# Reordering steps in a linear-attention and MLP block: tail scalings, low parts, hidden chunks and one `up` are issued at other places

## The chip, the cores and the metric

The kernel runs on one core of one Trainium2 chip, as a single program. The metric is the device time of one execution in microseconds (us); lower is better. The times of the kernel before are three executions, 745.16, 745.22 and 745.53 us, with a median of 745.22 us. One more execution was profiled.

## What is computed

One transformer block on 2048 tokens of width 640 (32 heads of 20), in float32:

```python
sa, ca, ga, sb, cb, gb = six rows of silu(c) @ w_mod
h = layernorm(x) * (1 + ca) + sa
x = x + ga * attention(h)          # below
h = layernorm(x) * (1 + cb) + sb
x = x + gb * (relu(h @ w1 + b1) ** 2 @ w2 + b2)     # w1: 640 x 1728

# attention: q, k, v = h @ wqkv, for each head
phi(t) = [softmax(t @ w_phi), softmax(-t @ w_phi)]
o = phi(q) (phi(k)^T v) / (phi(q) sum(phi(k)) + 1e-6),  then o @ wo
```

## The kernel before, in words

**Number format.** Each float32 operand of a large product is held as two parts in the matmul format: a high part (`hi`, an ACT copy that rounds) and a low part (`lo`, line 94: a DVE subtraction, original minus high part). A product is then three matmuls, high by high, high by low and low by high (`three`, line 91). So nearly every matmul operand is made by one ACT step and one DVE step after it, and PE waits for both.

**Stages.** (1) Up to about 248 us: weights are folded, layer norm, k, q and v are projected token tile by token tile, and `phi(k)^T v` is summed. (2) From there to 374 us: the query side, called the attention loop here, `for j in range(NB)` (line 1254), eight turns of 256 tokens each, that is two tiles of 128 tokens. (3) From 374 us to the end: the MLP, again eight turns `j` of 256 tokens (line 1666), each with seven inner turns `n` over pairs of 128-wide chunks of the hidden width 1728.

**The attention loop.** For each tile t of 128 tokens:

- `load_e` (line 899) reads the stored exponentials of the tile from DRAM, 640 KB, issued on SP's queue, into a buffer that an earlier tile must have left.
- `e_prod` (915): on DVE a product with the sums of phi(k) (line 919) and a reduction (921), then four small steps on POOL (924 to 928).
- `e_recip` (930): on DVE the reciprocal (933), which waits for the last POOL step, and one product (934).
- `e_scale` (961) is `e_tail` and then `e_main`. `e_tail` (938) scales the last two heads (line 944; on DVE for tiles 0 to 5, on POOL from tile 6 on). `e_main` (950) scales the other thirty heads on DVE (line 955).
- PE then does `tail_turn` (967: transposes of the tails into the single PSUM bank tagged `tp`), `tail_num` (974), `tr_e` (982: transposes of the main part) and `num` (992: products with the masked `phi(k)^T v`, in two banks and the `tp` bank), ACT takes the high parts (`num_hi`, 1010), and `num_lo` (1014) takes the low parts, from turn 2 on by DVE straight from PSUM (line 95 in the trace). The bank `tp` is free for the next `tail_turn` only after the last of those. `do_wo` (1027) is the output product, four pieces a turn (`i` the tile, `h` the half), of 15 matmuls each.

`todo_` and `turns` (1257 to 1262) say after how many matmuls of which piece of `do_wo` the steps of the next turn come in. PE, DVE, ACT and POOL run in the written order here; SP's order is left to the scheduler of the framework. Ahead of the loop lines 1224 to 1251 do the same for tiles 0 to 4 by hand; `kv_mask5` and `kv_masks` (889, 892) are DVE products that make the masked `phi(k)^T v`.

**Into the MLP.** `t2(0, d)` (1137) makes chunk d of the five chunks of `h` for the first 256 tokens: two ACT steps (lines 404 and 405) and one DVE subtraction (95). `prep` is one hidden weight: `p_hi`, an ACT copy (1083); `p_lo`, a DVE subtraction; `p_load`, the load of a later weight on SP. In the last turns of the attention loop they are issued in groups.

**The MLP.** `up(j, f)` (1362) is 15 matmuls into one of two banks, a relu on ACT (1380) and a square on DVE (1381). `split_a(j, n)` (1397) splits the squares of a pair into high (ACT, 1404 and 1410) and low parts (DVE); `down(0)` and `down(1)` multiply the pair before by w2 into the banks `acc` and `acc3x`. In a turn (j, n) the order on PE is `up(2n)`, `down(0)`, `up(2n+1)`, `down(1)`, where the downs are those of turn n-1. Between them stand calls of `prep` and `layer` (1643), which does the layer norm of the next 256 tokens in pieces; one of the pieces is `turn` (1172), a DVE transpose, after which `t2` of the next tokens can run. All engines are in the written order, SP too for j = 0.

Of the kernel before, what the change touches and what calls it, by code (L numbers as in the profile page):

```python
# [56 lines left out]
def kernel(  # L57
# [436 lines left out]
    def do_q(t, *between):  # L494
        q_out(t, proj("q", t, *between))
# [465 lines left out]
    def e_scale(t):  # L961
        e_tail(t)
        e_main(t)
# [151 lines left out]
    def p_lo(n=1):  # L1115
        for _ in range(n):
            if todo["lo"]:
                prep_lo(*todo["lo"].pop(0))

    def new(tag):  # L1120
        return lambda nm: wslot(nm, tag)

# [103 lines left out]
    e_prod(0)  # L1226
    e_prod(1)
    e_recip(0)
    e_scale(0)
    e_recip(1)  # L1230
    load_e(3)
    do_q(q0 + 2, (1, 0, kv_diags))
    e_tail(1)
    kv_mask5()
    e_main(1)
    kv_masks()
    e_prod(2)
# [6 lines left out]
    e_prod(3)  # L1244
    e_recip(2)
    e_recip(3)
    e_scale(2)
    load_e(5)
    e_scale(3)
    load_e(6)  # L1250
    e_prod(4)
    SPREAD, SUMS = {1: 1, 3: 2}, {3: 1, 4: 2}
# [1 line left out]
    for j in range(NB):  # L1254
        nxt = j + 1 < NB
        b, c = 2 * j + 5, 2 * j + 6
        turns = {1: ((0, 0, 11), (0, 0, 15), (0, 1, 4), (0, 1, 15)), 6: ((0, 1, 2), (0, 1, 8), (0, 1, 15), (1, 0, 15)),
                 0: ((0, 1, 4), (0, 1, 10), (1, 0, 3), (1, 0, 15))}.get(j, ((0, 0, 6), (0, 0, 11), (0, 0, 15), (0, 1, 15)))
        todo_ = (lambda: tail_turn(j + 1), lambda: tail_num(j + 1), lambda: tr_e(j + 1, range(3)), lambda: tr_e(j + 1, (3, 4)))

        def hooks(i, h):
            return [(at, f) for (i_, h_, at), f in zip(turns, todo_) if nxt and (i, h) == (i_, h_)]
        if j == 4:
            load_x1(0)
            load_dealt(0)
        if j < 5:
            p_load()
        if j == 5:
            q_chain(KEPT + 3, False)
        else:  # L1270
            e_prod(b)
        e_recip(b - 1)
        e_scale(b - 1)
        if j == 6:
            mod_sum(5, gate_b)
            spread_row(1, gb_b)
        load_e(b + 2)
        do_wo(j, 0, 0, *hooks(0, 0))
        if j - 1 in SPREAD:
            exps(EQ[KEPT + SPREAD[j - 1]])  # L1280
        if j == 5:
            exps(EQ[KEPT + 3])
            q_sums(KEPT + 3)
            e_prod(b)
        do_wo(j, 0, 1, *hooks(0, 1))
        if j == 7:
            t2(0, 0)
            t2(0, 1)
        if j == 4:
            ln0 = ln_dealt(0)  # L1290
            next(ln0)
            next(ln0)
        if j == 6:
            next(ln0)
            turn(0, 0)
            turn(0, 1)
        if 1 <= j < 6 and j != 4:
            p_hi()
        if j == 5:
            next(ln0)  # L1300
        if j in SUMS:
            q_sums(KEPT + SUMS[j])
        e_prod(c)
        if j != 5:
            e_recip(b)
            e_scale(b)
        do_wo(j, 1, 0, *hooks(1, 0))
        if j == 7:
            t2(0, 2)
            t2(0, 3)  # L1310
        if nxt:
            num(j + 1)
            num_hi(j + 1)
        if j == 4:
            next(ln0)
            next(ln0)
            next(ln0)
        if j == 5:
            p_hi()
        do_wo(j, 1, 1, b=8)  # L1320
        if j == 7:
            t2(0, 4)
        if not nxt:
            do_wo(j, 1, 1, a=8)
        if nxt:
            do_wo(j, 1, 1, a=8, b=11)
            num_lo(j + 1)
            do_wo(j, 1, 1, a=11)
        if j == 5:
            e_recip(b)  # L1330
            e_scale(b)
        if j in SPREAD:
            q_chain(KEPT + SPREAD[j], False)
        load_e(c + 2)
        if j:
            plus_x(j - 1)
        if j == 5:
            p_lo(4)
            p_load(4)
        if j == 6:  # L1340
            p_hi(4)
            p_lo(5)
            p_load(3)
        if j == 7:
            p_load(2)
    order.__exit__(None, None, None)


# [257 lines left out]
            out_(*r, u[:, at : at + m])  # L1606
            at += m

    def prep(n):
        p_hi(n)  # L1610
        p_lo(n)
        p_load(n)

    prev = None
    LN2 = {}

# [49 lines left out]
    for j in range(NB):  # L1666
        if j <= PLAIN:
            if j:
                by_hand.__exit__(None, None, None)
            by_hand = tc.manual_schedule(engines={ET_.PE, ET_.DVE, ET_.Activation, ET_.Pool} | ({ET_.SP} if j != 1 else set()))  # L1670
            by_hand.__enter__()
        for n in range(NP):
            down = lambda k: prev and (down_plain if plain(*prev) else down_pair)(*prev, k)
            twice = not plain(j, n)
            m = NP * j + n - NP - 1
            if (j, n) == (NB - 1, NP - 1):
                for k in range(2):
                    up(j, 2 * n + k)
                    split_a(j, n, (k,))
                break  # L1680
            done = j - 1 if j and prev else None
            up(j, 2 * n)
            if prev and not plain(*prev):
                split_s(*prev)
            down(0)
            if j < PLAIN:
                layer(j + 1, 2 * n, None if j else 0)
            if 0 < m < NP - 2:
                t_split(m - 1)
            if m == -1:  # L1690
                t_load(0)
            if (j, n) == (PLAIN, 0):
                t_fetch(4)
            if j >= PLAIN:
                if n == 5 + (j == PLAIN) - (j == NB - 1):
                    for i in range(2):
                        add_bias(j, i)
                layer(j + 1, 2 * n)
            prep(next(PREPS, 0))
            if j == 0:  # L1700
                layer(j + 1, 2 * n, 1)
# [24 lines left out]
            if j == NB - 1 and n == 1:  # L1726
                for k in range(NP - LAST, NP - 1):
                    plain_load(k)
            if j == NB - 1 and n == 3:
                for k in range(NP - LAST, NP - 1):  # L1730
                    plain_split(k)
            if j == NB - 1 and n == NP - 2:
                for i in range(2):
                    by_gate(Y[j][i], Y[j][i], slice(0, D))
                    add(Y[j][i], Y[j][i], XR[j, i])
            up(j, 2 * n + 1)
            if j >= PLAIN and n == 0:
                down(1)
            split_a(j, n)
            if twice:  # L1740
                sums(j, n)
            if j < PLAIN or n:
                down(1)
            if m == NP + 1:
                t_split(NP - 2)
            ahead = (j, n) == (0, 3)
            if ahead:
                layer(j + 1, 2 * n + 1)
            prep(next(PREPS, 0))
            if n == 0 and j:  # L1750
                end(j - 1, "4", 1, L)
                end(j - 1, "x", 1, R)
            if n == (2 if j > PLAIN else 1 if j == PLAIN else 0) and j:
                finish(j - 1, j >= PLAIN)
            if not ahead:
                layer(j + 1, 2 * n + 1)
            if (j, n) == (0, 4):
                nc.vector.tensor_tensor(bb, bb, gb_b, op=ALU.mult)
            if 0 <= m < NP - 2:
                t_sums(m)  # L1760
            if m == NP - 2:
                t_split(m - 1)
            if 0 < m + 1 < NP - 1:
                t_load(m + 1)
            if m == NP - 1:
                for i in range(2):
                    add_bias(j - 1, i)
            if j == NB - 1 and n == NP - LAST:
                first_combos(j)
            prev = j, n  # L1770
# [78 lines left out]
```

## Time and profile before

| | us |
|---|---|
| median of the timed executions | 745.22 |
| the profiled execution, its own time | 746.29 |
| its span, first to last instruction | 744.6 |
| PE busy | 735.9 |
| DVE busy | 600.1 |
| ACT busy | 453.6 |
| POOL busy | 168.3 |

The span is 1.7 us shorter than the profiled execution's own time, which in turn is 1.1 us above the median. PE, the engine of the matmuls, is busy for 99% of the span, and it is idle for the rest. In the rows of the profile, PE is the matmul, PEld its weight load, and a row of the timeline gives the start, the duration of a group of like instructions, the engine, the line of the kernel, what is written and read, and the count; brackets give the idle time of the engine before it and who ended it. Matmuls overlap, and their ends are modelled, so the distance from one start to the next is the surer figure.

### The profile page before, as it was taken

Reading aid. Unit: us, or ns where it says so; the run is one execution under the profiler, and the core shown is the slowest. Engines: PE = TensorE matmul, PEld = TensorE weight load, DVE = VectorE, ACT = ScalarE, POOL = GpSimd, SP = SyncE. Lnnn points to the kernel's source line nnn. Section 1 sums busy time; section 2 is a strip of 40 time slices with the busy share of each in tenths; the row PEclk is TensorE's granted clock in tenths of the full one; section 3 lists DMA queues with packets and bytes.
Section 4 is the critical chain, followed back from the end, with each engine's and each line's share of the span. In section 5 each row is a group of like instructions: output and inputs, shape, how many; then the busy total and the mean of one; then the engine's idle time right before and its main releaser. Section 6 shows DMA issues by size and latency. Waiting matters only on the chain.

```text
span 744.6 us, 16806 instructions
## 1 busy us (share of the span) xinstructions
PE 735.9 (99%) x6594; PEld 717.8 (96%) x6594; DVE 600.1 (81%) x1092; ACT 453.6 (61%) x1059; POOL 168.3 (23%) x357
## 2 busy tenths in 40 slices
PE   9999999999999999999999999999999999999997
PEld 8999999999999989988999999999999999999997
DVE  6598988988999999999666778877776776777765
ACT  5767666677853365666686567565664747557331
POOL 3000101001000357647203040231321313222110
PEclk9999999999999999999999999999999999999999
DMA  8912341333431345644984477997766777767451
GB/s 312 361 40 96 124 133 57 123 127 108 142 108 72 116 155 182 154 122 122 219 254 151 143 224 250 293 299 186 214 183 183 221 184 226 206 176 206 136 156 36
DMA packets 58421, 126.55 MB, mean 170 GB/s; under 512 B 7022, under 2 KB 16062, under 8 KB 58342
## 3 DMA queue, kind: packets, MB, share of 16 engines
q1 hardware_dynamic: 38110, 79.21, 32.5%
q0 software_dynamic: 17504, 40.90, 21.8%
q10 hardware_dynamic: 2727, 5.37, 1.9%
q8 instruction: 52, 0.85, 0.5%
q14 instruction: 28, 0.22, 0.1%
HBM read 100.80 MB, written 29.89 MB: 176 GB/s over the span
## 4 chain that ended last, share of the span: by engine, by line
PE 81%; DVE 10%; DMA 3%; POOL 2%; ACT 2%; issue 1%; SPq 0%; ACTq 0%; DVEq 0%; POOLq 0%
PE up L85 24%; PE acc L85 17%; PE pk L85 9%; PE pv L85 9%; PE pq L85 8%; PE acc3x L85 5%; PE pwo L85 3%; DVE dn L921 3%; DVE scr L919 2%; DVE ezb L955 2%; PE kvp L488 1%; DMA raw_q<-in_wq 1%; DMA xx<-a 1%; DMA ring_b<-td_b 1%; PE ta L393 1%
## 5 line engine op out<-in xcount | busy, mean ns | idle before, releaser
L85 PE MATMUL up<-h,w 128*128 128x256 f32 x1640 | 204.9, 277 | 0.1
L85 PEld LDWEIGHTS up<-h,w 128*128 128x128 f32 x1640 | 196.7, 188 | 0.7 <-DVE h L95 0.5
L1380 ACT ACTIVATE ft<-up,b_t 128x256 f32<-128x256 f32 x104 | 49.0, 471 | 96.9 <-PE up L85 96.6
L85 PE MATMUL acc<-w,ra 128*128 128x384 f32 x452 | 97.5, 335 | 0.0
L1381 DVE TENSOR_TENSOR ft<-ft 128x256 f32<-128x256 f32 x104 | 43.9, 422 | 42.9 <-ACT ft L1380 41.5
L85 PE MATMUL pwo<-wo,ot 128*128 128x384 f32 (+1 forms) x480 | 78.0, 313 | 0.0
L85 PE MATMUL pq<-wq,hT 128*128 128x384 f32 (+1 forms) x480 | 76.0, 313 | 0.0
L85 PE MATMUL pk<-wk,hT 128*128 128x384 f32 (+1 forms) x480 | 73.8, 310 | 0.0
L85 PEld LDWEIGHTS acc<-w,ra 128*128 128x128 f32 x452 | 72.7, 188 | 0.8 <-DVE ra L95 0.6
L85 PEld LDWEIGHTS pq<-wq,hT 128*128 128x128 f32 x480 | 71.5, 188 | 0.7 <-issue 0.5
L85 PEld LDWEIGHTS pwo<-wo,ot 128*128 128x128 f32 x480 | 69.5, 188 | 2.7 <-issue 2.7
L85 PE MATMUL pv<-wv,hT 128*128 128x384 f32 (+1 forms) x480 | 72.0, 307 | 0.0
L85 PEld LDWEIGHTS pk<-wk,hT 128*128 128x128 f32 x480 | 70.7, 188 | 1.2 <-DVE hT L95 0.7
L85 PEld LDWEIGHTS pv<-wv,hT 128*128 128x128 f32 x480 | 70.4, 188 | 0.0
L95 DVE TENSOR_TENSOR ra<-ft,ra 128x384 fp32r<-128x384 f32 (+2 forms) x86 | 36.9, 449 | 32.6 <-ACT ra L1404 19.4
L1490 POOL DMA_DIRECT2D ring_a<-td_a x34 | 18.5, 543 | 116.5 <-PE acc L85 106.3
L1404 ACT ACTIVATE ra<-ft 128x384 fp32r<-128x384 f32 x48 | 25.2, 526 | 28.4 <-DVE ft L1381 22.4
L85 PE MATMUL acc3x<-w,ra 128*128 128x256 f32 x231 | 39.5, 278 | 0.0
L85 PEld LDWEIGHTS acc3x<-w,ra 128*128 128x128 f32 x231 | 37.2, 188 | 0.0
L479 DVE TENSOR_REDUCE sk<-ek 128x64 f32<-128x1280 f32 x16 | 23.7, 1484 | 13.4 <-ACT ek L474 9.1
L1395 DVE TENSOR_TENSOR ft<-ft 128x128 f32<-128x128 f32 x136 | 33.3, 287 | 1.2
L370 POOL TENSOR_SCALAR sma<-sma 128x2 f32<-128x2 f32 x6 | 2.3, 376 | 132.8 <-ACT xb L369 132.8
(264 smaller groups left out, 1443.9 us busy)
## 6 DMA issues: line engine op xcount, KB each, us to landing
ring_c<-td_c POOLq DMA_DIRECT2D x34, 384.0 KB, 3.9
ring_a<-td_a POOLq DMA_DIRECT2D x34, 384.0 KB, 3.4
ring_b<-td_b POOLq DMA_DIRECT2D x34, 256.0 KB, 3.4
esp<-eq SPq DMA_DIRECT2D x12, 640.0 KB
el<-esp SPq DMA_DIRECT2D x12, 640.0 KB
rw<-in_w SPq DMA_DIRECT2D x23, 320.0 KB
wm<-in_w_mod SPq DMA_DIRECT2D x20, 320.0 KB
xb<-in_x SPq DMA_DIRECT2D x8, 640.0 KB
```

The source lines that it names most:

```text
L85: nc.tensor.matmul(o, a, b, start=first and i == 0, stop=last and i == len(terms) - 1, skip_group_check=skip,)
L95: (eng or nc.vector).tensor_tensor(out_lo, full, hi.bitcast(F32), op=ALU.subtract)
L393: nc.tensor.transpose(p[:, i * P : (i + 1) * P], src, ident)
L479: nc.vector.tensor_reduce(s, heads(flat(e)), axis=AX.X, op=ALU.add)
L919: nc.vector.tensor_tensor(z, flat(ET[t]), flat(zb), op=ALU.mult)
L921: nc.vector.tensor_reduce(dn.rearrange("p s h -> p (s h)"), heads(z), axis=AX.X, op=ALU.add)
L955: nc.vector.tensor_tensor(EU[t][:, :, :120].rearrange("p u (s h d) -> p s u h d", s=2, d=DH), ET[t][:, :, :600].rearrange("p s (u h d) -> ...
L1380: nc.scalar.activation(r, p, AF.Relu, bias=b1_t[:, f : f + 1])
L1381: nc.vector.tensor_tensor(r, r, r, op=ALU.mult)
L1395: nc.vector.tensor_tensor(t[:, o], t[:, a], t[:, b], op=op)
L1404: nc.scalar.activation(a[:, 0, :3], t[:, :3], AF.Copy)
L1490: nc.gpsimd.dma_start(RING[j, n, r], TD[n][r].bitcast(F32R))
```

## The change

Six groups of edits, all of them of order; no instruction is added or taken away.

1. Tiles 0 and 1: `e_tail(0)`, `kv_mask5` and `e_tail(1)` come ahead of `e_main(0)`; `load_e(3)`, which takes the buffer that `e_main(0)` reads, comes after it.
2. Tiles 2 and 3: both tails come ahead of both mains.
3. Turn j = 4 of the attention loop: `e_main(13)` comes after `num_lo(5)` and not ahead of it. In the other turns the lines are written anew with the same order.
4. `t2(0, 0)` comes at the end of turn 6, each of the other chunks one piece of `do_wo` sooner in turn 7, the last one ahead of the last piece. One of the weights (high part, low part) and one load go from the end of turn 6 to the end of turn 7.
5. MLP, turn (0, 1): `up(0, 3)` comes ahead of `down(0)`.
6. MLP, turn (0, 5): one `prep` comes after the relu of `up(0, 11)`; turn (0, 4): the piece of `layer` (a `turn`) comes ahead of a `prep`.

```diff
@@ tiles 0 to 3 @@
     e_recip(0)
-    e_scale(0)
+    e_tail(0)
+    do_q(q0 + 2, (1, 0, kv_diags))
+    kv_mask5()
     e_recip(1)
+    e_tail(1)
+    e_main(0)
     load_e(3)
-    do_q(q0 + 2, (1, 0, kv_diags))
-    e_tail(1)
-    kv_mask5()
     e_main(1)
...
     e_recip(3)
-    e_scale(2)
+    e_tail(2)
+    e_tail(3)
+    e_main(2)
     load_e(5)
-    e_scale(3)
+    e_main(3)
@@ attention loop @@
         do_wo(j, 0, 0, *hooks(0, 0))
+        if j == 7:
+            t2(0, 1)
...
         if j == 7:
-            t2(0, 0)
-            t2(0, 1)
+            t2(0, 2)
+            t2(0, 3)
...
             e_recip(b)
-            e_scale(b)
+            e_tail(b)
+            if j != 4:
+                e_main(b)
         do_wo(j, 1, 0, *hooks(1, 0))
         if j == 7:
-            t2(0, 2)
-            t2(0, 3)
+            t2(0, 4)
...
-        do_wo(j, 1, 1, b=8)
-        if j == 7:
-            t2(0, 4)
...
+        do_wo(j, 1, 1, b=11)
         if nxt:
-            do_wo(j, 1, 1, a=8, b=11)
             num_lo(j + 1)
-            do_wo(j, 1, 1, a=11)
+        if j == 4:
+            e_main(b)
+        do_wo(j, 1, 1, a=11)
...
         if j == 6:
-            p_hi(4)
-            p_lo(5)
-            p_load(3)
+            p_lo()
+            t2(0, 0)
+            p_hi(3)
+            p_lo(3)
+            p_load(2)
         if j == 7:
-            p_load(2)
+            prep(1, 3)
@@ MLP @@
             up(j, 2 * n)
+            ahead = (j, n) == (0, 1)
+            if ahead:
+                up(j, 2 * n + 1)
...
-            prep(next(PREPS, 0))
+            parts = next(PREPS, 0)
+            late_ = (j, n) == (0, 5)
+            if not late_:
+                prep(parts)
...
-            up(j, 2 * n + 1)
+            if not ahead:
+                up(j, 2 * n + 1)
...
+            if late_:
+                prep(parts)
             split_a(j, n)
...
-            ahead = (j, n) == (0, 3)
-            if ahead:
+            sooner = (j, n) in ((0, 3), (0, 4))
+            if sooner:
                 layer(j + 1, 2 * n + 1)
```

More of the change, by code (lines that the diff above doesn't have):

```diff
@@ L1118, in p_lo, with prep @@
                 prep_lo(*todo["lo"].pop(0))
+    def prep(n, m=None):
+        p_hi(n)
+        p_lo(n)
+        p_load(n if m is None else m)
     def new(tag):
@@ L1319 @@
             p_hi()
-        do_wo(j, 1, 1, b=8)
-        if j == 7:
-            t2(0, 4)
-        if not nxt:
-            do_wo(j, 1, 1, a=8)
+        do_wo(j, 1, 1, b=11)
         if nxt:
-            do_wo(j, 1, 1, a=8, b=11)
             num_lo(j + 1)
-            do_wo(j, 1, 1, a=11)
+        if j == 4:
+            e_main(b)
+        do_wo(j, 1, 1, a=11)
         if j == 5:
@@ L1607, in last_downs @@
             at += m
[L1609 to L1612, printed above, removed]
     prev = None
@@ L1754 @@
                 finish(j - 1, j >= PLAIN)
-            if not ahead:
+            if not sooner:
                 layer(j + 1, 2 * n + 1)
```

## The prediction, made before the changed kernel was run

> **What bounds the kernel now.** I read the page first, then who PE's weight loads waited for between 236 and 420 us (the stretch that the change touches), then busy times by window, then the timeline engine by engine around each of PE's waits.
>
> ```profile
> span 744.6 us, 16806 instructions
> PE 735.9 (99%) x6594; PEld 717.8 (96%) x6594; DVE 600.1 (81%) x1092; ACT 453.6 (61%) x1059; POOL 168.3 (23%) x357
> PE 81%; DVE 10%; DMA 3%; POOL 2%; ACT 2%; issue 1%; SPq 0%; ACTq 0%; DVEq 0%; POOLq 0%
> ```
>
> PE is busy for 99% of the span, and yet a tenth of the chain that ended last runs over DVE. Both are true: there is a stretch where DVE has no pause either and PE is only just not held up. The second view says what ended the pauses of the weight loads, the third where DVE is full.
>
> ```profile
> PEld tail L971 <- DVE ut L944: 1.1, 2, 0.8
> PEld tail L971 <- POOL rn L1195: 0.9, 1, 0.9
> ...
> 248.27:309.44 61.17, 60.62 (x451) 54.66 (x450) 59.09 (x71) 31.78 (x73) 34.73 (x62) 1.00 0.51 158
> 309.44:338.42 28.98, 28.53 (x214) 25.55 (x212) 28.22 (x33) 17.88 (x41) 15.14 (x30) 1.00 0.58 138
> ```
>
> In the window rows the fifth number is DVE's busy time: 59.1 of 61.2 us, then 28.2 of 29.0. So from 248 to 338 us the query side runs at DVE's pace, and a wait of PE taken away there comes back at the next place where PE needs DVE, unless DVE itself gets that result ready sooner. That is the question for edits 1 to 3. After 374 us PE sets the pace, and there a wait taken away stays away.
>
> **Edits 1 and 2, tails of tiles 0 to 3 ahead of the mains.** PE's rows around the four tail transposes:
>
> ```profile
> 256.74 0.27 PE L971 MATMUL tail<-ident,ut 128*80 128x128 f32 x1
> 257.45 0.31 PE L971 MATMUL tail<-ident,ut 128*80 128x128 f32 x1 [0.44 <-DVE ut L944]
> 268.36 0.69 PE L971 MATMUL tail<-ident,ut 128*80 128x128 f32 x2
> ...
> 309.60 0.38 PE L971 MATMUL tail<-ident,ut 128*80 128x128 f32 x2
> ```
>
> An undisturbed pair takes 0.38 us, its second start 0.38 - 0.27 = 0.11 after the first. At 257 us the second came 0.71 after the first: 0.60 lost. At 268 us the pair took 0.69: 0.31 lost. With both tails in front of the mains (1.40 us each, below) both are ready in time, and PE gains 0.9 us here.
>
> Does it keep them? The next tails in front of which PE has little room come with turn 2, where the transposes need the bank `tp`, which DVE's third low part frees:
>
> ```profile
> 309.03 0.41 DVE L95 TENSOR_TENSOR ot<-numc,ot 128x256 fp32r<-128x256 f32 x1
> ...
> 306.67 3.10 PE L85 MATMUL pwo<-wo,ot 128*128 128x256 f32 x21
> ...
> 334.88 3.09 PE L85 MATMUL pwo<-wo,ot 128*128 128x256 f32 x21
> 338.57 0.39 PE L971 MATMUL tail<-ident,ut 128*80 128x128 f32 x2 [0.60 <-DVE ot L95]
> ...
> 335.44 1.45 DVE L955 TENSOR_TENSOR ezb<-eq,dn 128x1200 f32<-128x1200 f32 x1
> 338.01 0.41 DVE L95 TENSOR_TENSOR ot<-numc,ot 128x256 fp32r<-128x256 f32 x1
> ```
>
> At 338 us, where PE surely waited, it started 338.57 - 338.42 = 0.15 after the low part's end. At 309 us the low part ended at 309.44, so PE could start at 309.59, and it did at 309.60. PE waited there for nothing, but with a room of 0.01 us. A PE that comes 0.9 us earlier waits 0.9 there. DVE is not sooner, since the edits leave it the same work and it goes from one step to the next without a pause. So I cost edits 1 and 2 at no gain, and ask how much later they make DVE:
>
> ```profile
> 252.94 0.59 POOL L928 TENSOR_TENSOR dd<-dd,dn 128x32 f32<-128x32 f32 x2
> 254.69 1.78 POOL L928 TENSOR_TENSOR dd<-dd,dn 128x32 f32<-128x32 f32 x2
> ...
> 254.96 1.40 DVE L955 TENSOR_TENSOR ezb<-el,dn 128x1200 f32<-128x1200 f32 x1
> 256.50 0.35 DVE L933 RECIPROCAL dd<-dd 128x32 f32<-128x32 f32 x1
> ```
>
> The reciprocal of tile 1 waits for POOL's pair of additions. The pair took 0.59 us for tile 0, with DVE in a reduction, and 1.78 for tile 1, from 254.69 to 256.47, when `e_main(0)` ran beside it from 254.96 to 256.36. With `e_main(0)` moved behind the reciprocal, the pair should take 0.59 and end at 255.28, so the reciprocal starts about 1.2 us sooner and `e_main(0)` 1.2 later. DVE, free of the first tail at 254.96, then waits until 255.28, 0.32 us less the small mask product that now lies in between, where it waited 0.14 before (256.36 to 256.50). So it comes between nothing and 0.2 later; I take 0.1. The Trainium skill (SBUF — State Buffer, "Who interferes with whom") says that a VectorE instruction with two SBUF inputs and a GpSimd one that reads SBUF lock each other out, whichever starts first holding the port to its end; by that rule the second addition is held by `e_main(0)`, as the row has it, and comes free by the edit. If the slow pair had another cause, DVE would stand 1.2 us more, which is a rival below.
>
> SP: `load_e(3)` now waits for `e_main(0)` in its later place.
>
> ```profile
> 256.39 2.78 SPq L905 DMA_DIRECT2D el<-esp  x2
> 256.40:260.40 4.00, 3.56 (x30) 3.24 (x30) 3.83 (x7) 0.96 (x4) 0.58 (x3) 1.00 0.63 192
> ...
> 262.34 1.48 DVE L919 TENSOR_TENSOR scr<-el,zb 128x1280 f32<-128x1280 f32 x1
> ```
>
> It was issued at 256.39, when `e_main(0)` ended, and will be at about 257.6. In the 4.00 us behind the issue 192 GB/s x 4.00 = 768 KB moved, more than its 655 KB (128 x 1280 x 4 bytes), so I let it take 4 us: there at 261.6, and needed at 262.34. The cover is 0.7 us. If it is gone, every us counts on DVE's chain. The other loads are issued well ahead of use.
>
> **Edit 3, low part ahead of the scaling in turn 4.** From the product group `pwo` to the tails is 309.60 - 306.67 = 2.93 us undisturbed and 338.57 - 334.88 = 3.69 at 338 us: 0.76 lost, because `e_main(13)` stood in front of the low parts. With it behind, they end about 1.4 us sooner, at 337.0; PE could start at 337.2 and comes at 338.57 - 0.76 = 337.81. The whole 0.76 goes, with 0.6 us to spare. Next in line is `e_main(13)`: it ends where the low parts ended, and PE needs it only behind the tail steps that follow 338.57. Edits 1 to 3 together: 0.76 - 0.10 = **0.65 us**.
>
> **Edit 4, the chunks of `h`.** Rows of PE, then of ACT and DVE:
>
> ```profile
> 374.19 6.44 PE L85 MATMUL up<-h,w 128*128 128x256 f32 x45
> 380.47 1.01 PE L85 MATMUL acc<-w,ra 128*128 128x384 f32 x3
> ...
> 382.54 1.86 PE L85 MATMUL up<-h,w 128*128 128x256 f32 x15
> 384.24 0.68 PE L85 MATMUL acc<-w,ra 128*128 128x384 f32 x3
> ...
> 366.58 1.37 ACT L1083 ACTIVATE w<-rawt 128x640 fp32r<-128x640 f32 x2 [0.40 <-ACT at L1051]
> 370.09 0.39 ACT L1051 ACTIVATE at<-pwo 128x256 f32<-128x256 f32 x1 [0.52 <-PE pwo L85]
> ...
> 376.12 0.43 DVE L95 TENSOR_TENSOR h<-xm,h 128x256 fp32r<-128x256 f32 x1 [0.52 <-ACT h L405]
> ```
>
> One `up` takes 384.24 - 382.54 = 1.70 us, three 5.10; the first three took 380.47 - 374.19 = 6.28. Of the 1.18 us more I count **1.0** as waits for chunks 3 and 4 and the rest as a slightly slower pace of 45 matmuls. The fifth chunk's low part was ready at 376.55; PE needs it 13 matmuls after its start, at 374.19 + 13 x 1.70 / 15 = 375.66. ACT gets one weight copy less ahead of it (0.65 us, from 1.37 for two) and fills the 0.52 us in which it waited for PE with a chunk: 1.15 sooner, 375.4. That is 0.25 us in front of the need. Bounds: 0.7 if the chunk still comes 0.3 late, 1.18 if the pace goes too. The moved copy stands in front of the first relu; the moved load of an MLP weight is issued some us later, with two loads of the next tokens behind it on SP, all used some us after that.
>
> **Edit 5, `up(0, 3)` ahead of the first downs.** The first product group took 1.01 us instead of 0.68: **0.33** lost on the split of the first pair. It now comes a whole `up`, 1.70 us, later.
>
> ```profile
> 378.91 0.47 ACT L1380 ACTIVATE ft<-up,b_t 128x256 f32<-128x256 f32 x1 [0.60 <-PE up L85]
> ...
> 380.43 0.76 DVE L95 TENSOR_TENSOR ra<-ft,ra 128x384 fp32r<-128x384 f32 x2 [0.59 <-ACT ra L1404]
> ```
>
> But edit 4 has PE here a us earlier. From the relu's start to the end of the low part are 381.19 - 378.91 = 2.28 us. The second `up` ends at 374.19 + 3.40, so relu about 377.8, low part 380.1; the fourth `up` ends at 374.19 + 6.80 = 380.99. Covered by 0.9 us, and by 0.2 with the moved copy (0.65) all in front.
>
> **Edit 6.** At 415 us the same wait:
>
> ```profile
> 413.35 1.86 PE L85 MATMUL up<-h,w 128*128 128x256 f32 x15
> 415.17 1.03 PE L85 MATMUL acc<-w,ra 128*128 128x384 f32 x3
> ...
> 412.64 0.72 ACT L1083 ACTIVATE w<-rw 128x640 fp32r<-128x640 f32 x1
> 413.27 0.45 ACT L1380 ACTIVATE ft<-up,b_t 128x256 f32<-128x256 f32 x1
> 414.59 0.52 ACT L1404 ACTIVATE ra<-ft 128x384 fp32r<-128x384 f32 x1 [0.87 <-DVE ft L1381]
> ```
>
> 415.17 - 413.35 = 1.82 instead of 1.70, and 1.03 instead of 0.68: **0.47** lost. The relu comes 0.63 sooner without the copy, which fits into the 0.87 us that ACT then waits for the square; the earlier transpose in turn (0, 4) brings the chunks in front of it forward as well. All of the 0.47 goes.
>
> **The sum** is 0.65 + 1.0 + 0.33 + 0.47 = 2.45; I take 2.4 us. Against the profiled execution's own 746.29 (span 744.6) that makes 743.9, a span of 742.2. The profile lies 1.1 above the median, so for timed executions 745.22 - 2.4 = **742.8 us**. A measurement of this kernel can tell about 0.2%, 1.5 us, from no change.
>
> **Rivals.** (a) PE keeps the 0.9 us of edits 1 and 2, because DVE's wait-free rows hide a reserve, as in POOL steps slowed by DVE: 2.45 + 0.1 + 0.9 = 3.4, 741.8 us. For it: the releases at 309 us are inferred from one row. Against it: the room of 0.01 us. (b) POOL's additions stay slow: DVE 1.2 us later, attention a loss of 0.5, the rest as above: 1.3 us, 743.9. Against it: 0.59 for the pair beside a reduction. (c) In the MLP ACT falls behind: its copies wait for late loads, or the first relu for the moved copy, so that half of edits 4 to 6 comes back as waits at the next downs: 0.65 + 0.9 = 1.55, 743.7. For it: margins of 0.2 us. (d) Slower: SP's order is not written out. If it puts the two weight loads `rawt` (128 x 640 x 4 bytes, 328 KB each) in front of `load_e(3)`, that tile lands when 655 + 655 KB have moved from 259.33 on at 296 GB/s (the rate of the next stretch), 4.4 us, and what was fixed in the 4.0 above, 4.0 - 655 / 296 = 1.8: at 265.5, 3.2 us after DVE wants it, and DVE's whole chain to 338 us shifts.
>
> ```profile
> 259.33 1.46 SPq L1073 DMA_DIRECT2D rawt<-in_w  x2
> ...
> 260.40:264.50 4.10, 4.10 (x38) 2.96 (x35) 4.03 (x4) 3.83 (x9) 1.83 (x3) 1.00 0.80 296
> ```
>
> 3.2 against 2.45 makes it 0.75 us slower, 746.0; it is slower from a landing at 262.34 + 2.45 = 264.8 on, and by over 0.2% from 266.3 on. Against it: those two loads were released 3 us after `e_main(0)` ended.
>
> **How the numbers follow.** The forecast has 0.60, (a) 0.15, (b) 0.07, (c) 0.14, (d) 0.04. The forecast's own bounds are 2.0 (chunk late by 0.3, DVE later by 0.2) to 2.8. For 8 in 10 the range takes in (a) and most of (c): 741.7 to 743.9. Faster by over 0.2% are the forecast, (a) and not quite half of (b) and (c): 0.84. Within 0.2%: 0.13. Slower by over 0.2%, a part of (d): 0.03.
>
> **What would show it.** The pair of tail transposes at 257 and 268 us takes 0.4 us; PE gets a new wait of up to 0.9 us for a low part at about 309.7, and none at 337.9. DVE's row of scalings at 256 us is 1.2 later, POOL's pair of additions 0.6 long. The first `up`s take 5.1 to 5.3 us, and the first products 0.68 at about 380 and 412. Wrong I would be if the wait at 309 us is missing and PE is 0.9 us ahead there, if DVE pauses at 262 us for the load, or if new waits of `acc` come up between 384 and 415 us.

## The result, and the profile after

The changed kernel takes 741.99 us in the median of six runs (741.57 to 742.70), the kernel before 745.64 us (six runs, 745.16 to 747.42). The ratio is 0.995, with a 95% interval from 0.9937 to 0.9963: faster, by 3.65 us, where 2.4 were forecast. In two later sets the same two kernels lay 2.75 us apart (742.85 against 745.60, ratio 0.9962, 0.9949 to 0.9976) and 2.78 us (742.44 against 745.22, ratio 0.9967, 0.9954 to 0.998).

The profiled execution has a span of 741.0 us against 744.6 and took 742.70 us against 746.29. The page counts one instruction more than before, 16807 against 16806; the numbers of busy instructions on the five rows of engines are the same. First the page, its head and the chain that ended last; then the busy times of the same two windows that the prediction shows of before (the fifth number is DVE's busy time).

```profile
span 741.0 us, 16807 instructions
PE 734.7 (99%) x6594; PEld 717.9 (97%) x6594; DVE 599.2 (81%) x1092; ACT 454.0 (61%) x1059; POOL 169.0 (23%) x357
PE 86%; DVE 9%; DMA 3%; issue 1%; ACT 0%; POOL 0%; SPq 0%; DVEq 0%; ACTq 0%
```

```profile
248.27:309.44 61.17, 60.91 (x456) 55.19 (x456) 59.05 (x73) 32.22 (x74) 32.79 (x60) 1.00 0.52 161
309.44:338.42 28.98, 28.59 (x216) 25.72 (x215) 28.26 (x34) 17.87 (x41) 14.49 (x30) 1.00 0.56 132
```

DVE is as full as before, 59.05 of 61.17 and 28.26 of 28.98 us: the change takes nothing off it. The places named in the prediction come next, PE's timeline first.

```profile
257.55 0.38 PE L971 MATMUL tail<-ident,ut 128*80 128x128 f32 x2
...
268.56 0.38 PE L971 MATMUL tail<-ident,ut 128*80 128x128 f32 x2
...
282.13 0.27 PE L971 MATMUL tail<-ident,ut 128*80 128x128 f32 x1
282.66 0.31 PE L971 MATMUL tail<-ident,ut 128*80 128x128 f32 x1 [0.26 <-DVE ut L944]
...
309.30 0.69 PE L85 MATMUL pwo<-wo,ot 128*128 128x384 f32 x3
310.37 0.39 PE L971 MATMUL tail<-ident,ut 128*80 128x128 f32 x2 [0.39 <-DVE ot L95]
...
335.57 3.02 PE L85 MATMUL pwo<-wo,ot 128*128 128x256 f32 x21
338.44 0.38 PE L971 MATMUL tail<-ident,ut 128*80 128x128 f32 x2
...
374.06 7.23 PE L85 MATMUL up<-h,w 128*128 128x256 f32 x60
381.13 0.69 PE L85 MATMUL acc<-w,ra 128*128 128x384 f32 x3
...
412.00 1.86 PE L85 MATMUL up<-h,w 128*128 128x256 f32 x15
413.70 0.68 PE L85 MATMUL acc<-w,ra 128*128 128x384 f32 x3
```

Read them against the rows of before:

- At 257 and 268 us both pairs take 0.38 us, as an undisturbed one does: the 0.60 and 0.31 us that were lost there are won.
- At 282 us the second transpose now starts 0.53 us after the first, 0.42 more than the 0.11 of an undisturbed pair. At 310 us three matmuls of 384 columns start at 309.30; such a group of three takes 0.51 (413.70 to 414.21, where the next group starts), so the pair could have started at 309.81 and started at 310.37: 0.56 lost. Together 0.98. So the 0.91 us that edits 1 and 2 won at 257 and 268 us are given back.
- At 338 us the pair follows the product group after 338.44 - 335.57 = 2.87 us, where it took 3.69: no wait. On DVE the low part that frees the bank ends at 337.31 + 0.41 = 337.72, ahead of the scaling; PE could have started 0.15 us later, at 337.87, and came at 338.44. The room is 0.57 us, forecast 0.6.
- Four up-projections take 381.13 - 374.06 = 7.07 us, 1.77 each, and the first products 0.69 without a wait. So three take 5.30 instead of 6.28, and the slower pace that the forecast left out of its 1.0 us is still there (5.30, not 5.10). The fifth chunk's low part ends at 374.72 + 0.43 = 375.15; by the forecast's reckoning PE needs it at 374.06 + 13 x 1.70 / 15 = 375.53, 0.38 us later (forecast 0.25).
- At 412 us the up-projection takes 413.70 - 412.00 = 1.70 us and its products 0.68: no wait.

The two rows of DVE that this used, then DVE and POOL around 256 us:

```profile
337.31 0.41 DVE L95 TENSOR_TENSOR ot<-numc,ot 128x256 fp32r<-128x256 f32 x1
...
374.72 0.43 DVE L95 TENSOR_TENSOR h<-xm,h 128x256 fp32r<-128x256 f32 x1 [0.89 <-ACT h L405]
```

```profile
256.08 0.35 DVE L933 RECIPROCAL dd<-dd 128x32 f32<-128x32 f32 x1 [0.16 <-POOL dd L928]
256.46 0.23 DVE L934 TENSOR_TENSOR dn<-rs_q,dd 128x64 f32<-128x64 f32 x1
256.72 0.24 DVE L944 TENSOR_TENSOR ut<-el,dn 128x80 f32<-128x80 f32 x1
256.88 2.72 DVE L955 TENSOR_TENSOR ezb<-el,dn 128x1200 f32<-128x1200 f32 x2
```

```profile
255.46 0.59 POOL L928 TENSOR_TENSOR dd<-dd,dn 128x32 f32<-128x32 f32 x2
```

POOL's pair of additions took 0.59 us instead of 1.78, now that no scaling runs beside it, and DVE paused 0.16 us for it, as before (0.14).

The load of tile 3, on SP's queue, and the product that needs it:

```profile
258.31 1.65 SPq L905 DMA_DIRECT2D el<-esp  x2
260.01 0.90 SPq L1073 DMA_DIRECT2D rawt<-in_w  x2
...
263.13 1.48 DVE L919 TENSOR_TENSOR scr<-el,zb 128x1280 f32<-128x1280 f32 x1
```

The load goes out ahead of the two weight loads, and DVE does not pause for it. When it was there can be read from the DMA packets that start between its issue and 262.0 us, and between its issue and 267.5 us:

```profile
DMA packets 161, 0.75 MB, mean 204 GB/s; under 512 B 16, under 2 KB 16, under 8 KB 160
DMA packets 577, 1.98 MB, mean 216 GB/s; under 512 B 64, under 2 KB 64, under 8 KB 576
```

The second stretch holds the packets of all four loads issued here (1.98 MB, for two of 655 KB and two of 328), and 64 of them are small, 16 for each load. The first 16 small ones have started by 261.96, and no other follows before 263.3. Taken as the end of the first load, they put it 3.65 us behind its issue (the forecast let it take 4.0) and 1.17 us ahead of the product (forecast 0.7).

To see where the time went I cut every profile at six of PE's starts: the first matmul of the group `z` (line 857), the tail transposes at 338 us, the first up-projection, two matmuls of up-projections at about 413 and 421 us, and one in the last of them; the end of the span closes the last stage. Every entry is the difference of two starts. The last three marks are the same matmuls of `up` in every kernel, counted in order: the one at 413 us begins an up-projection, the one at 421 us is the sixth matmul of one that starts 0.57 us earlier (420.14 before, 418.27 after), and the last mark is the fifth matmul from the end of the last one.

| kernel | first `z` at | z to 338 | to first up | to 413 | to 421 | to last up | to the end |
|---|---|---|---|---|---|---|---|
| before | 245.20 | 93.37 | 35.62 | 39.16 | 7.35 | 311.53 | 12.34 |
| before, second | 245.30 | 93.53 | 35.66 | 39.18 | 7.32 | 311.77 | 10.71 |
| edits 1, 2 | 244.63 | 93.54 | 35.96 | 39.09 | 7.29 | 312.20 | 10.70 |
| edit 3 | 245.10 | 92.63 | 35.93 | 39.08 | 7.35 | 311.33 | 10.71 |
| edit 4 | 245.15 | 93.40 | 35.96 | 38.32 | 7.31 | 311.52 | 10.71 |
| edits 5, 6 | 245.00 | 93.39 | 35.83 | 38.84 | 6.84 | 311.08 | 10.71 |
| edits 4 to 6 | 244.81 | 93.52 | 35.82 | 37.92 | 6.84 | 311.31 | 11.80 |
| after | 246.04 | 92.40 | 35.62 | 37.94 | 6.84 | 311.44 | 10.71 |
| after, second | 245.91 | 92.63 | 35.80 | 37.90 | 6.84 | 311.74 | 10.71 |
| after, third | 245.01 | 92.67 | 35.64 | 37.94 | 6.84 | 312.43 | 10.71 |
| low parts in turns 1 to 4 | 245.71 | 92.56 | 35.65 | 37.90 | 6.84 | 311.24 | 10.71 |
| low parts in turns 2, 4 | 245.60 | 91.90 | 35.73 | 37.91 | 6.84 | 311.62 | 10.71 |
| the same, and tail of tile 5 | 244.56 | 92.06 | 35.86 | 37.90 | 6.84 | 312.42 | 10.70 |

Two columns, to 413 and to 421, show the change in steps far larger than their scatter. In z to 338 the step is 0.9 us, and kernels with the same order there scatter by 0.2 us (old) and 0.3 to 0.4 (new). The others scatter without regard to the change: 1.5 us ahead of `z`, 0.3 from 338 us to the first up, 1.35 between 421 us and the last up, 1.6 at the end.

### The profile page after: what moved, and what is told of

Same layout as the page of the kernel before. It is cut to its first block, busy times and chain, and to the rows that moved or that the text cites. A ratio compares the mean times of both kernels' runs of the same rounds, so it can differ in the third digit from the quotient of the medians.

```text
span 741.0 us, 16807 instructions
## 1 busy us (share of the span) xinstructions
PE 734.7 (99%) x6594; PEld 717.9 (97%) x6594; DVE 599.2 (81%) x1092; ACT 454.0 (61%) x1059; POOL 169.0 (23%) x357
## 4 chain that ended last, share of the span: by engine, by line
PE 86%; DVE 9%; DMA 3%; issue 1%; ACT 0%; POOL 0%; SPq 0%; DVEq 0%; ACTq 0%
PE up L85 25%; PE acc L85 18%; PE pv L85 9%; PE pk L85 9%; PE pq L85 8%; PE pwo L85 6%; PE acc3x L85 5%; DVE dn L921 2%; DVE scr L919 2%; DVE ezb L955 2%; DMA xb<-in_x 2%; PE kvp L488 1%; PE te L989 1%; PE ta L393 1%; DMA raw_q<-in_wq 1%; DMA raw_k<-in_wk 1%
```

## The experiments

The theory on trial is the forecast's: to 338 us DVE sets the pace, so a wait of PE that is taken away there comes back unless DVE delivers sooner; from 374 us on PE sets it and waits taken away stay away. The rivals: PE keeps what it gains in both stages; or ACT, or POOL, gives part of it back.

**The kernel before again**, with no edit.

> The kernel before, unchanged, for a second profiled execution. If the 0.84 us by which the first z matmul came later after the change, and the 1.63 us by which the last store's end came sooner behind the last computation, are variation from execution to execution, this profile shows either of them moved by some tenths of a microsecond up to 1.5 us against the first profile of the same kernel (first z matmul at 245.20, last store's end 4.39 behind the last computation). If they are effects of the change, both stand within 0.1 us of those values.

One run took 745.45 us, and its profile has the first `z` at 245.30 but the stretch from the last up-projection to the end at 10.71, where the first profile of the same kernel had 12.34. So the 1.63 us at the end are variation: nearly every other profile has 10.7. They lie behind the last computation, a DVE step that ends 4.38 us before the span does in the first profile and 2.75 us before it in the second. The start varied little between these two, but over the thirteen of the table it lies between 244.56 and 246.04, without order by kernel. Of the 3.59 us between the two first spans, 1.63 are thus not the change's; the 0.84 us at the start went the other way.

**Edits 1 and 2 alone**

```diff
-    e_scale(0)
+    e_tail(0)
...
+    e_tail(1)
+    e_main(0)
...
-    e_scale(2)
+    e_tail(2)
+    e_tail(3)
+    e_main(2)
```

> Edits 1 and 2 alone (the small tails of tiles 0 to 3 ahead of the large scalings). Forecast's theory, VectorE sets the pace to 338 us: the two TensorE waits at 257 and 268 us (0.9 us together) are gone, come back as TensorE waits at about 282 and 310 us (0.5 each), the wait before the last tail turn at about 338 stays, and the first up-projection comes within -0.1 to +0.1 us of where it was, counted from the first z matmul. Rival, TensorE keeps what it gains: no new waits, 0.9 us sooner there.

745.22 us against 745.32, ratio 0.9999 (0.999 to 1.0007): nothing. PE's timeline shows it place by place:

```profile
280.83 0.27 PE L971 MATMUL tail<-ident,ut 128*80 128x128 f32 x1
281.48 0.31 PE L971 MATMUL tail<-ident,ut 128*80 128x128 f32 x1 [0.38 <-DVE ut L944]
...
307.73 1.22 PE L85 MATMUL pwo<-wo,ot 128*128 128x384 f32 x6
309.19 0.39 PE L971 MATMUL tail<-ident,ut 128*80 128x128 f32 x2 [0.24 <-DVE ot L95]
...
336.32 1.22 PE L85 MATMUL pwo<-wo,ot 128*128 128x384 f32 x6
338.17 0.39 PE L971 MATMUL tail<-ident,ut 128*80 128x128 f32 x2 [0.63 <-DVE ot L95]
```

At 281 us 281.48 - 280.83 - 0.11 = 0.54 are lost, at 309 us 309.19 - 307.73 - 2 x 0.51 = 0.44, together 0.98, and the wait at 338 us, which the edits don't touch, is still there. From `z` to 338 us it takes 93.54 us, against a mean of 93.44 for the five kernels with the old code there (93.37, 93.53, 93.40, 93.39, 93.52): 0.1 more, as forecast, but within their scatter. PE doesn't keep the 0.9 us.

DVE's own steps are a better mark here than `z`. Its first product behind `z` (line 919, at 248.27 us in the profile before) starts 3.00 to 3.29 us after `z`, varying from profile to profile. Counted from that product, the transposes at 310 us start after 61.31 to 61.36 us in all eleven profiles that have the old order in turn 2, of the kernel before, of the edits alone and of the changed kernel. The low part at 338 us ends after 90.12 to 90.18 us in the six with the old order in turn 4, and this run's 90.14 is one of them. So edits 1 and 2 make DVE no later that can be seen; the 0.1 us between the means is the place of `z`.

**Edit 3 alone**

```diff
-            e_scale(b)
+            e_tail(b)
+            if j != 4:
+                e_main(b)
...
             num_lo(j + 1)
+            if j == 4:
+                e_main(b)
```

> Edit 3 alone (the low parts of tile 5 ahead of the scaling of tile 13). Forecast's theory: the TensorE wait before the last tail turn at about 338 us goes, the first up-projection comes 0.76 us sooner counted from the first z matmul, and the waits at 257 and 268 stay (0.9 us together). Rival, part of the 0.97 us that the whole change won in the attention stage needs edits 1 and 2: then this one brings clearly less, 0.4 us or under.

744.31 us against 745.32, ratio 0.9988 (0.9979 to 0.9997). From `z` to 338 us 92.63 us, 0.81 less than 93.44; the pair at 338 us follows its product group without a wait:

```profile
334.80 3.09 PE L85 MATMUL pwo<-wo,ot 128*128 128x256 f32 x21
337.73 0.38 PE L971 MATMUL tail<-ident,ut 128*80 128x128 f32 x2
```

That is 2.93 us between the starts, the 2.93 that the prediction took for undisturbed. This edit alone brings nearly all that the whole change brings in the attention stage (the three profiles of the changed kernel: 92.40, 92.63, 92.67, mean 92.57, 0.87 less). It makes DVE deliver sooner: counted from DVE's first product, the low part at 338 us ends after 88.64 us here and 88.67 to 88.70 in the changed kernel, against 90.12 to 90.18. Edits 1 and 2 don't. On PE, the stretch from the transposes at 310 us to those at 338 takes 28.20 us here and 28.07 to 28.21 in the changed kernel, against 28.93 to 29.00 with the old order.

**Edits 4, 5 and 6 alone**, with the attention as before but for the chunks that edit 4 moves in its last turns.

```diff
         if j == 7:
-            t2(0, 0)
-            t2(0, 1)
+            t2(0, 2)
+            t2(0, 3)
...
+            if ahead:
+                up(j, 2 * n + 1)
...
-            ahead = (j, n) == (0, 3)
+            sooner = (j, n) in ((0, 3), (0, 4))
```

> Edits 4, 5 and 6 alone; attention as before. Forecast's theory: nothing moves ahead of the first up-projection (within 0.1 us, counted from the first z matmul), and from there to the last computation the kernel is 1.7 to 1.9 us faster (1.0 for the chunks, 0.3 for the up-projection ahead, 0.5 for the relu ahead of the copy). Rival, ScalarE falls behind later in the MLP stage: half of it comes back, 0.9 us. If the parts of the whole change add, this with tails_only and low_only gives 2.5 to 2.8 us.

743.45 us against 745.32, 1.87 less, ratio 0.997 (0.9959 to 0.9982). From the first up to 413 us 37.92 us instead of a mean of 39.13 in the four profiles with the old code there (39.16, 39.18, 39.09, 39.08), 1.21 less, and 6.84 instead of a mean of 7.32 (7.35, 7.32, 7.29, 7.35 and 7.31) to 421 us, 0.48 less: 1.69. Nothing of it is given back by 421 us, and behind it this kernel has 311.31 us, at the lower end of the scatter. Over all profiles that stretch has a mean of 311.7 us with any of edits 4 to 6 and of 311.7 without. That ACT falls behind later does not show.

The medians of these three kernels, 0.10, 1.01 and 1.87 us below before, add to 2.98, a little over the 2.5 to 2.8 expected; the changed kernel, timed in other sets, lies 2.75 and 2.78 below. By their steps in the traces the three add to -0.10 + 0.81 + 1.69 = 2.40.

**Edit 4 alone**

```diff
+        if j == 7:
+            t2(0, 1)
...
         if j == 7:
-            t2(0, 0)
-            t2(0, 1)
+            t2(0, 2)
+            t2(0, 3)
...
+            t2(0, 0)
+            p_hi(3)
+            p_lo(3)
```

> Edit 4 alone (chunks of h an output product sooner; the fourth up-projection and the relu stay where they were). Forecast's theory: 1.0 us less at the first up-projections, but the first down-projections then wait for the split of their input, which cannot follow as fast: 0.3 to 0.6 us of it is given back at about 380 us, so 0.4 to 0.7 us are left at the last computation. Rival, the three edits are independent: the whole 1.0 us is left.

744.70 us against 745.60, ratio 0.9993 (0.9984 to 1.0003), so the time by itself cannot tell it from no change; PE's timeline can:

```profile
374.51 5.46 PE L85 MATMUL up<-h,w 128*128 128x256 f32 x45
379.81 1.02 PE L85 MATMUL acc<-w,ra 128*128 128x384 f32 x3
380.67 0.51 PE L85 MATMUL acc3x<-w,ra 128*128 128x256 f32 x3
...
387.00 0.79 PE L85 MATMUL acc<-w,ra 128*128 128x384 f32 x3
```

The three ups take 379.81 - 374.51 = 5.30 us instead of 6.28: 0.98 won. The first products take 1.02, a wait of 0.33 as before the change (1.01), no longer. I had expected 0.3 to 0.6 us more there, since the split of their input could not follow; but the relu and the split came sooner by as much as the ups did: the relu of the second up starts 3.74 us behind the first up instead of 4.72, and the low parts end 6.02 behind it instead of 7.00. Only 0.11 shows in the third product group, 0.79 instead of 0.68. Up to 413 us 39.13 - 38.32 = 0.81 of the 0.98 are left. That lies between my 0.4 to 0.7 and the rival's whole 1.0. The mechanism that I gave here, a longer wait at the first products, is not there.

**Edits 5 and 6 alone**

```diff
+            ahead = (j, n) == (0, 1)
+            if ahead:
+                up(j, 2 * n + 1)
...
+            late_ = (j, n) == (0, 5)
+            if not late_:
+                prep(parts)
...
-            ahead = (j, n) == (0, 3)
+            sooner = (j, n) in ((0, 3), (0, 4))
```

> Edits 5 and 6 alone (the fourth up-projection ahead of the first down-projections; a relu ahead of a copy). Forecast's theory: 0.33 and 0.47, so 0.8 us sooner at the last computation, the first up-projections with the waits they had. Rival: the up-projection ahead fills a stretch in which TensorE would have waited anyway only once the chunks come sooner: 0.5 us, from the relu alone.

744.23 us against 745.60, ratio 0.9982 (0.9972 to 0.9992). To 413 us 39.13 - 38.84 = 0.29, to 421 us 7.32 - 6.84 = 0.48, together 0.77: the forecast's sum of 0.8, not the rival's 0.5. The first products now find their input:

```profile
374.22 8.20 PE L85 MATMUL up<-h,w 128*128 128x256 f32 x60
382.26 0.68 PE L85 MATMUL acc<-w,ra 128*128 128x384 f32 x3
...
413.07 1.86 PE L85 MATMUL up<-h,w 128*128 128x256 f32 x15
414.77 0.68 PE L85 MATMUL acc<-w,ra 128*128 128x384 f32 x3
```

**The changed kernel again**, twice, with no edit.

> The changed kernel again, with a second profile. Theory, the measured 3.65 us holds about 2.8 us of the change's own work and 0.8 of variation outside of it: against before 2.4 to 3.0 us in the stages from the first z matmul to the last computation, and a median that lies 2.4 to 3.7 us under before. Rival, the change also moves the end of the last store: the stretch from the last computation to the end is again near 2.76 us, against 4.39 before.

> The changed kernel again, timed beside the variants of it. Theory: 2.4 to 3.0 us under before in the median, 128.0 to 128.5 us from the first z matmul to the first up-projection; the kernel with turns 2 and 4 lies 0.4 to 0.55 us under it by the trace, which the medians may not tell apart.

742.85 and 742.44 us; 128.43 and 128.31 us from `z` to the first up (128.02 in the first profile), and 10.71 at the end both times. The two medians lie 2.75 and 2.78 us under before. The end of 10.71, which the rival ascribed to the change, is what the kernel before has in its second profile too.

**Low parts ahead of the scaling in turns 1 to 4.** With edits 1 and 2 paid back at 282 and 310 us, the wait at 310 could perhaps be taken away as edit 3 did at 338.

```diff
-            if j != 4:
+            if not 1 <= j <= 4:
                 e_main(b)
...
-        if j == 4:
+        if 1 <= j <= 4:
             e_main(b)
```

> The changed kernel with the large scaling behind the low parts in turns 1 to 4, not in turn 4 alone. Theory, the wait of 0.55 us at 310 us is the scalings ahead of what the tail turn needs, and before the last tail turn VectorE has room of 0.57 us: the wait goes and the first up-projection comes 0.5 us sooner than in the changed kernel. Rival, the sum of VectorE's work sets the time at 338: the wait moves there and nothing is won.

742.32 us, ratio 0.9963 (0.9951 to 0.9976); 92.56 us from `z` to 338, against 92.57 for the changed kernel: nothing won, as the rival had it. But DVE's timeline shows another reason than a sum that is the same in any order:

```profile
293.00 0.69 DVE L95 TENSOR_TENSOR ot<-numb,ot 128x512 fp32r<-128x512 f32 x1 [0.17 <-ACT ot L1012]
...
320.33 0.69 DVE L95 TENSOR_TENSOR ot<-numa,ot 128x512 fp32r<-128x512 f32 x1 [0.41 <-ACT ot L1012]
321.19 0.69 DVE L95 TENSOR_TENSOR ot<-numb,ot 128x512 fp32r<-128x512 f32 x1 [0.17 <-ACT ot L1012]
```

In turns 1 and 3 the low parts came up before ACT's copy was done, and DVE stood idle for 0.75 us that the scaling in front of them used to fill. At 338 us PE then waits again:

```profile
338.27 0.39 PE L971 MATMUL tail<-ident,ut 128*80 128x128 f32 x2 [0.21 <-DVE ot L95]
```

**Low parts ahead in turns 2 and 4.** In turn 2 of that run DVE did not pause, so there the swap should cost nothing.

```diff
-            if j != 4:
+            if j not in (2, 4):
                 e_main(b)
...
-        if j == 4:
+        if j in (2, 4):
             e_main(b)
```

> The changed kernel with the large scaling behind the low parts in turns 2 and 4, not in turn 4 alone. Theory from the run with turns 1 to 4: there VectorE stood idle 0.17 us at 293 and 0.42 and 0.17 us at 320 and 321, since the low parts came up before ScalarE's copy of their input, and those 0.76 us came back as a wait at 338; in turn 2 it did not stand. So with turns 2 and 4 alone the wait of 0.55 us at 310 goes, VectorE keeps its times, no wait comes at 338 (room 0.7 us), and the first up-projection comes 0.4 to 0.55 us sooner than in the changed kernel, counted from the first z matmul. Rival, VectorE's sum sets 338 whatever its order: no gain.

From `z` to 338 us 91.90 us, 0.67 less than the changed kernel's mean; to the first up 127.63 against 128.25 (128.02, 128.43, 128.31), 0.62 less, a little more than the 0.4 to 0.55 expected. PE passes 309 and 338 us without a wait:

```profile
309.46 0.38 PE L971 MATMUL tail<-ident,ut 128*80 128x128 f32 x2
...
337.50 0.38 PE L971 MATMUL tail<-ident,ut 128*80 128x128 f32 x2
```

```profile
336.90 0.41 DVE L95 TENSOR_TENSOR ot<-numc,ot 128x256 fp32r<-128x256 f32 x1
```

The low part ends at 337.31. At 338 us in the kernel before, where PE waited, it started 0.15 us behind such an end, so here it could start at 337.46. It starts at 337.50, so the 0.7 us of room that I had counted on are used up. The time is 741.82 us, beside 742.44 for the changed kernel in the same set; the intervals against before, 0.9942 to 0.9972 and 0.9954 to 0.998, overlap. It beats the kernel before beyond doubt; that it beats the changed kernel rests on the trace, one profile against three (four with the late load below), and on a difference of the medians of 0.62 that agrees with it.

**The same, with the tail of tile 5 sooner**

```diff
+        if j == 0:
+            e_recip(b)
+            e_tail(b)
         e_prod(c)
         if j != 5:
-            e_recip(b)
-            e_tail(b)
+            if j:
+                e_recip(b)
+                e_tail(b)
```

> As the kernel with turns 2 and 4, and in turn 0 the reciprocal and the tail of tile 5 ahead of the product of tile 6, so that the wait of 0.48 us at 282 goes too. Theory: two waits of 1.03 us together are gone, but at 338 VectorE's low parts then end last: of the 1.03 us some 0.7 are won against the changed kernel, and a wait of 0.2 to 0.5 us shows at 338 (more if VectorE has to wait for GpSimd's additions of tile 5, which end at 278.9). Rival, TensorE alone sets the time from there: 1.0 us won, no wait at 338.

92.06 us to 338: not better than 91.90, and 741.92 us. The wait at 282 us is gone (the pair takes 0.38 us there), and it comes back twice further on, in PE's timeline:

```profile
294.43 0.39 PE L971 MATMUL tail<-ident,ut 128*80 128x128 f32 x2 [0.23 <-DVE ot L95]
...
336.62 0.39 PE L971 MATMUL tail<-ident,ut 128*80 128x128 f32 x2
```

```profile
336.06 0.41 DVE L95 TENSOR_TENSOR ot<-numc,ot 128x256 fp32r<-128x256 f32 x1
```

At 338 us PE starts 0.15 after the low part's end, 336.47: held up by DVE, as the expectation said, though I had looked for 0.7 us against the changed kernel, and it is 0.51. The rival, 1.0 us, is out. The low part itself comes 336.47 - 244.56 = 91.91 us after `z`, and without the tail's move 337.31 - 245.60 = 91.71. DVE is 0.20 us later, 0.15 of it by what it now pauses for POOL's additions at 277.54. So DVE's work sets 338 us, and which waits of PE stand before it is without effect.

**The load of tile 3 later**

```diff
-    load_e(3)
     e_main(1)
     kv_masks()
+    with tc.issue_after(newest(ET_.DVE)):
+        load_e(3)
```

> The changed kernel with the load of tile 3 issued later, behind the scaling of tile 1 instead of that of tile 0, some 1.5 to 2.5 us later than 258.31. Forecast's theory: the load takes 4.0 us and is needed at 263.13, with a cover of 0.84 us; the product of tile 3 then waits 0.7 to 1.7 us on VectorE, and since VectorE sets the pace to 338 us the first up-projection comes as much later, 0.7 to 1.7 us less what room there is (0.1 to 0.7). Rival, the cover is larger or VectorE is not the bound: within 0.2 us of the changed kernel.

742.05 us, within the scatter of the changed kernel. But it is no test of the cover, since the load did not go later in SP's queue:

```profile
257.91 1.64 SPq L905 DMA_DIRECT2D el<-esp  x2
```

That is 12.56 us after this profile's first `z` (245.35), and in the changed kernel it was 258.31 - 246.04 = 12.27. The two scalings run from 256.48 for 2.72 us here, so the first ended at about 257.9: the load still went out as soon as it had ended, and not behind the second. What a late load costs stays open. The run counts as a fourth profile of the changed kernel: 92.80 from `z` to 338 (with it the mean is 92.63, 0.82 less than before), 37.91 from the first up to 413 and 6.84 to 421. Read as above from the packets, the load was there 3.90 us behind its issue, 0.93 ahead of its use; over all profiles with edits 1 and 2 it took 3.45 to 4.26 us and was 0.56 to 1.37 ahead.

## Why the prediction was right, point by point

- **Edits 1 and 2, at no gain, 0.1 later.** Right that nothing is gained. The 0.1 us of cost does not show: alone they add 0.10 us from `z` to 338, which DVE's own steps put down to the place of `z`, and with edit 3 they take nothing away (0.81 for edit 3 alone, 0.87 with all three). The mechanism was the one named: what is won at 257 and 268 us is waited for later. The place was only half right. I named 309 us with its room of 0.01; the trace has the wait at 282 too, for the tail of tile 5, 0.42 of the 0.98. My rows had skipped it: the pair at 282 us had no wait before, and I had not asked how much room it had.
- **POOL's additions.** 0.59 us, as forecast, against 1.78; the scaling starts 10.84 us behind `z` instead of 9.76, 1.08 later (forecast 1.2). The rule of the Trainium skill (SBUF — State Buffer, "Who interferes with whom") that I had weighed gives the same, and the trace agrees: the pair was slow beside the scaling, fast without it. Rival (b) is out.
- **The load.** In the changed kernel it was issued at 258.31, and as `z` came 0.84 later, that is 257.47 in the times of before (forecast 257.6). DVE did not pause for it. Rival (d) is out: SP sent it ahead of the two weight loads. By the packets the cover was 1.17 us, against 0.7 forecast; what happens without it no run shows.
- **Edit 3, 0.76.** Measured alone 0.81; together with 1 and 2 0.87, against 0.65. That is the largest miss of the sum, 0.2 us. About 0.1 is the cost of edits 1 and 2 that did not come; the rest is within the scatter of this stage (0.27 among the three profiles of the changed kernel). From 310 to 338 us alone edit 3 brings 0.77.
- **Edit 4, 1.0.** 0.98 over the first three ups, with the chunk ready in time and the slower pace left; 0.81 up to 413 us when alone.
- **Edit 5, 0.33.** 0.29 alone. In the changed kernel edits 4 and 5 together come to 39.13 - 37.93 = 1.20, against 1.33: 0.13 short.
- **Edit 6, 0.47.** 0.48.
- **The sum.** 0.87 + 1.20 + 0.48 = 2.55, against 2.45. That it fits to 0.1 is in part luck: the misses of 0.2 and 0.13 have opposite signs.
- **The time.** 742.8 was forecast; 741.99, 742.85 and 742.44 were measured, in the range each time. The first set's 3.65 us is 1.1 over the traced 2.55. No wait in the traces explains these 1.1, and two repeats don't show them: 2.75 and 2.78. The stages that the change does not touch scatter by 1.5, 1.35 and 1.6 us from one profile to the next, and the kernel before alone ranged from 744.16 to 747.60. I take them for that; it is argued and not shown. What the two repeats have over 2.55, 0.2 us, is below what they can tell.
- **Rivals (a) and (c).** (a) is out by the run of edits 1 and 2: no 0.9 us is kept. The first set's 741.99 by itself would have spoken for (a), with its 741.8, rather than for 742.8. (c) is out up to 421 us: with the edits the columns to 413 and 421 are shorter in every profile and equal within 0.04 us.

## What to carry to other kernels

Where an engine beside PE has hardly a pause over a stretch (here DVE, 59.05 of 61.17 us), removing a wait of PE may only move it, as it did here; ask which edit makes that engine deliver sooner at the end of the stretch, and cost only that one. Before a step is moved ahead on such an engine, look whether its input is already there: the same swap won 0.8 us in turn 4 and 0.6 in turn 2, where the input was ready, and it idled the engine for 0.75 us in turns 1 and 3, where it was not. And when a change is worth a few us, cut the traces at fixed points and compare stage by stage: 0.3 us could be seen there, where the medians of whole runs moved by 0.4 us (before) and 0.9 (changed) from set to set.

## What I had not expected of the hardware

The stages that no edit touched are not equally steady. From the last up-projection to the end took 10.70 to 10.71 us in most profiles, but 12.34 and 11.80 in two; the difference lies behind the last computation (4.38 and 3.84 us instead of 2.75), and what made it is open. From 421 us to the last up-projection it varied between 311.08 and 312.43, and part of that has a name: in the third profile of the changed kernel, in PE's waits from 440 us on, one load into `ring_b`, which the down-projections `acc` read from DRAM's `td_b`, came late:

```profile
PE acc L85 <- DMA ring_b<-td_b: 1.0, 1, 1.0
```

In the second profile it was 0.2 us, and in the first none shows among PE's own waits. The two other profiles with more than 312 us in that stage show such waits too, 0.8 us for `ring_b` (edits 1 and 2 alone, 312.20) and 0.4 for `ring_a` (the tail of tile 5, 312.42); the rest have 0.3 at most. So the same kernel, with the same instructions, loses up to 1 us to one DMA in one execution and nothing in the next.
